# Retention then bilinear FFN: the query and key transposes of chunks 9 to 35 move from SP's DMA queue to the TensorE

## The chip, the core and the metric

One core of one Trainium2 chip. The metric is device microseconds of one execution, the median of several runs: 366.49 us for the kernel before (three runs, 366.24 to 366.78). Engines are named as the profile names them: PE is the TensorE (matmuls), PEld its weight loads, DVE the VectorE, ACT the ScalarE, POOL the GpSimd, SP the SyncE, whose queue only issues DMAs here.

## What is computed

A retention layer without softmax, then a bilinear feed-forward layer (FFN):

```python
# q, k, v: [8 batches, 8 heads, 576 positions, 64], float32
scores = 1/8 * q @ k^T                       # per batch and head
Dmat[h, i, j] = gamma_h ** (i - j) if i >= j else 0,  gamma_h = 1 - 2 ** (-5 - h)
x = ((scores * Dmat) @ v)  -> [4608 tokens, 512]      # heads side by side
out = ((x @ w_a) * (x @ w_b)) @ w_out        # 512 -> 1536 -> 512, float32
```

## The kernel before

The 4608 tokens are 36 chunks of 128. Two batches of 576 positions make nine chunks, so every fifth chunk is shared by two batches. The decay is split into a factor for the query (`qs`) and one for the key position (`vs`), so that a chunk needs only a causal mask and a running state `kv` of keys times values.

A chunk goes through these steps. `load` (L97) fetches q, k and v by SP DMAs. `cast` (L182) makes bf16 copies: q and k into the halves of one tile `qkb`, and v times `vs` into `vb` (L193). From chunk 4 on `cast` is called from `ahead`; for chunks 0 to 8 q and k are cast on ACT and DVE (L188, L189), for chunks 9 to 35 on POOL (L191, L192). The scores need q and k with the head dimension on the partitions, `qkT`. For chunks 0 to 8 `transposes` (L208) makes it on PE: eight 128x128 transposes into a PSUM tile `tp` (L213), whose halves ACT and DVE copy out (L217, L218). For chunks 9 to 35 `turn` (L200) makes it with one DMA transpose on SP's queue (L203). `state` (L225) adds keys times values to `kv` on PE (L236), and ACT copies the two diagonal blocks out (L241, L242). `scores` (L244) makes two PSUM tiles on PE (L253); the mask multiplication into `sT` on DVE (L259) is not issued at once but put in the list `later`. `outputs` (L267) multiplies `sT` and the state with `vb` and `qkT` on PE (L276, L285); the multiplication with `qs` into `xT` on DVE (L291) is put in `later` as well.

The FFN (`ffn_block`, L299) works on blocks of 512, 256, 384, 384 and then six times 512 tokens. For each of 12 column groups F it makes `pa` (L309, 4 matmuls, copied out by ACT as `ha`, L315) and `pb` (L322, 4 matmuls, multiplied by `ha` on DVE into `hT`, L327); then for each chunk of the block `po` (L335, 12 matmuls of 512 columns), copied out by ACT or DVE as `osb` (L344, L346) and stored by SP (L347). `pa`, `pb` and `po` share three PSUM buffers; `tp`, the scores and `o` share four.

The order of all instructions is written out by hand. `ffn_block` is a generator that yields after each matmul with a cost in units of one 512-column matmul; after each `pb` and at three places of each `po` it allows other work. After each `pb` and twice in each `po` it also calls `pop`, which issues one entry of `later`. A list `todo` of steps with due times in the same unit is worked off at these places. For chunks 9 to 35, taken in pairs, the due times are placed back from the block that needs the result (`starts`): `third` is at least 16 units ahead of it and 60 ahead of the next pair's. In the kernel before, `ahead` is due 104 units ahead of `third` (not before 176) and issues the casts of the pair, the loads of two chunks four further on, and the two DMA transposes; `first_stage` (`state` of the first chunk) 16 ahead of `second`; `second_stage` (`state` of the other and `scores` of both) 36 ahead of `third`, or 26 for chunks 9 and 10. Chunks 4 to 8 have their own times. At the end of each FFN block `flush` issues all that is left in `later`.

Of the kernel before, what the change touches and what calls it, by code (L numbers as in the profile page):

```python
# [11 lines left out]
BF16 = mybir.dt.bfloat16  # L12
# [6 lines left out]
def kernel(  # L19
# [19 lines left out]
    nc = tc.nc  # L39

    B, H, S, D = q.shape
    DM = H * D
# [4 lines left out]
    HP = H // 2  # L47
# [9 lines left out]
    def rows_of(i):  # L57

        b, m = 2 * (i // PER), i % PER
        if m < MID:  # L60
            return [(0, 128, b, 128 * m)]
        if m == MID:
            return [(0, 64, b, 128 * m), (64, 64, b + 1, 0)]
        return [(0, 128, b + 1, 64 + 128 * (m - MID - 1))]

    def pool(name, bufs, space=None):
        kw = {} if space is None else {"space": space}
        return ctx.enter_context(tc.tile_pool(name=name, bufs=bufs, **kw))
# [2 lines left out]
    big = pool("big", 1)  # L71
    stage = pool("stage", 5)
    nat = pool("nat", 5)
    qkt_pool = pool("qkt", 6)
    st_pool = pool("st", 4)
    h_pool = pool("hT", 2)
    ha_pool = pool("ha", 6)
# [19 lines left out]
    def load(i):  # L97
        if i >= NCH:
            return
        tiles = []  # L100
        for name, src in (("qf", q), ("kf", k), ("vf", v)):
            t = stage.tile([128, DM], FP32, tag=name, name=name)
            for r0, n, b, s0 in rows_of(i):
                nc.sync.dma_start(
                    t[r0:r0 + n, :].rearrange("p (h d) -> p h d", h=H),
                    src[b, :, s0:s0 + n, :].rearrange("h s d -> s h d"))
            tiles.append(t)
        staged[i] = tiles
# [62 lines left out]
    natural, transposed, kv_of, state_of, scored = {}, {}, {}, {}, {}  # L171
# [9 lines left out]

    def cast(i, early=False):  # L182
        qf, kf, vf = staged.pop(i)
        qkb = nat.tile([128, 2, DM], BF16, tag="qkb", name="qkb")
        vb = nat.tile([128, DM], BF16, tag="vb", name="vb")
        qb, kb = qkb[:, 0], qkb[:, 1]
        if early:
            nc.scalar.copy(qb, qf)  # L188
            nc.vector.tensor_copy(kb, kf)  # L189
        else:  # L190
            nc.gpsimd.tensor_copy(qb, qf)  # L191
            nc.gpsimd.tensor_copy(kb, kf)  # L192
        nc.gpsimd.tensor_tensor(  # L193
            vb.rearrange("p (h d) -> p h d", h=H),
            vf.rearrange("p (h d) -> p h d", h=H),
            vs[:, i % PER, :].unsqueeze(2).to_broadcast([128, H, D]),
            op=ALU.mult)
        natural[i] = (qkb, qb, kb, vb)

    def turn(i):  # L200

        qkT = qkt_pool.tile([128, 2, HP, 128], BF16, tag="qkT", name="qkT")
        nc.sync.dma_start_transpose(  # L203
            qkT.rearrange("p w c s -> p (w c) s"),
            natural[i][0].rearrange("p w d -> p (w d)"))
        transposed[i] = qkT

    def transposes(i, how):  # L208
        qkb, qb, kb, vb = natural[i]
        tp = ps_att.tile([128, 2, HP, 128], BF16, tag="att", name="tp")  # L210
        for w, src in ((0, qb), (1, kb)):
            for p in range(HP):
                nc.tensor.transpose(tp[:, w, p, :],  # L213
                                    src[:, p * 128:(p + 1) * 128], identity)
        qkT = qkt_pool.tile([128, 2, HP, 128], BF16, tag="qkT", name="qkT")
        if how == "both":
            nc.scalar.copy(qkT[:, 0], tp[:, 0])  # L217
            nc.vector.tensor_copy(qkT[:, 1], tp[:, 1])  # L218
        elif how == "act":
            nc.scalar.copy(qkT, tp)  # L220
        else:
            nc.vector.tensor_copy(qkT, tp)
        transposed[i] = qkT

    def state(i):  # L225
        m = i % PER
        if m == PER - 1:
            return
        qkb, qb, kb, vb = natural[i]
        r = slice(64, 128) if m == MID else slice(0, 128)  # L230
        if m == 0 or m == MID:
            kv_of[0] = ps_kv.tile([128, HP, 128], FP32, tag="kv", name="kv")
        kv = kv_of[0]
        for p in range(HP):
            sl = slice(p * 128, (p + 1) * 128)
            nc.tensor.matmul(kv[:, p, :], kb[r, sl], vb[r, sl],  # L236
                             start=(m in (0, MID) and p == 0), stop=True,
                             skip_group_check=True)
        st = states[i % len(states)]
        state_of[i + 1] = st  # L240
        nc.scalar.copy(st[0:64, :, 0:64], kv[0:64, :, 0:64])  # L241
        nc.scalar.copy(st[64:128, :, 64:128], kv[64:128, :, 64:128])  # L242
# [23 lines left out]

    def outputs(i):  # L267
        m = i % PER
        qkb, qb, kb, vb = natural.pop(i)
        qkT = transposed.pop(i)  # L270
        sT = scored.pop(i)
        o = ps_att.tile([128, HP, 128], FP32, tag="att", name="o")
        for p in range(HP):
            for hi in (0, 1):
                e0 = p * 128 + 64 * hi
                nc.tensor.matmul(o[64 * hi:64 * hi + 64, p, :],  # L276
                                 vb[:, e0:e0 + 64], sT[:, hi, p, :],
                                 start=(p == 0), stop=(m == 0),
                                 skip_group_check=True)
        if m > 0:  # L280
            st = state_of.pop(i)
            n = 64 if m == MID else 128
            for p in range(HP):
                for hi in (0, 1):
                    nc.tensor.matmul(o[64 * hi:64 * hi + 64, p, 0:n],  # L285
                                     st[:, p, 64 * hi:64 * hi + 64],
                                     qkT[:, 0, p, 0:n],
                                     start=False, stop=True,
                                     skip_group_check=True)
        s0 = rows_of(i)[0][3]  # L290
        later.append(lambda: nc.vector.tensor_tensor(  # L291
            xT[:, :, i * 128:(i + 1) * 128], o, qs[:, :, s0:s0 + 128],
            op=ALU.mult))
# [60 lines left out]
    make_qs(0)  # L354
    make_qs(1)
    cast(0, early=True)
    make_qs(2)
    for i in range(4):
        transposes(i, "both")
        if i == 0:  # L360
            make_qs(3)
        scores(i)
        state(i)
        flush()
        if i < 3:
            if i == 2:
                load_w(0, 128 * WCOLS[0])
            cast(i + 1, early=True)
        outputs(i)
        flush()  # L370
# [19 lines left out]
        at += total(n)  # L390

    counts = {"cast": 4, "load": 8}
    FIRST_TURNED = 9

    def ahead(upto, early=False):
        while counts["cast"] <= min(upto, NCH - 1):
            i = counts["cast"]
            cast(i, early)
            counts["cast"] += 1
            if counts["load"] < NCH:  # L400
                load(counts["load"])
                counts["load"] += 1
            if i >= FIRST_TURNED:
                turn(i)

    def first_stage(g):
        state(g[0])

    def second_stage(g):
        for i in g[1:]:  # L410
            state(i)
        for i in g:
            scores(i)

    def third_stage(g):
        flush()
        for i in g:
            outputs(i)

    def one_by_one(what, i):  # L420
        if what == "T":
            ahead(i, early=True)
            transposes(i, "both")
        elif what == "S":
            scores(i)
            state(i)
        else:
            flush()
            outputs(i)

    todo = []
    limit = 1e9
    for i in range(NCH - 1, 8, -2):
        g = (i, i + 1) if i + 1 < NCH else (i,)
        third = min(starts[i] - 16, limit - 60)
        limit = third
        second = third - (26 if i == 9 else 36)
        todo += [(max(176, third - 104), ahead, (g[-1],)),
                 (second - 16, first_stage, (g,)),
                 (second, second_stage, (g,)),  # L440
                 (third, third_stage, (g,))]
    for i, first, second, third in (
            (4, 117, 122, 129), (5, 134, 138, 143), (6, 147, 151, 158),
# [46 lines left out]
```

## Time and profile before

| | before |
|---|---|
| median of three runs | 366.49 us |
| the profiled execution's own time | 366.24 us |
| its span, first to last instruction | 364.5 us |
| PE busy | 335.3 us, 92% of the span |
| DVE, ACT, POOL busy | 164.0, 115.1, 77.5 us |
| mean granted PE clock | 0.99 |
| DMA transposes on SP's queue | 27, issued from 83.6 to 296.5 us |

A row of the profile's groups names line, engine, operation and tiles, then the busy time, the mean duration of one in ns, and after a bar the time that the engine sat idle before them with what ended that. Durations of matmuls overlap, since they are pipelined: what one costs in a stream is the distance from its start to the next one's, not its duration. In a timeline a row is the start, the time until the last of its instructions ends, and the instructions.

The profile divides at some 97 us. Ahead of that loads, casts and the first chunks wait for each other (PE is busy for 74 of 97 us, by its pipelined count). After that PE runs the FFN with the steps of the other chunks between its matmuls, up to 361 us, when the last copy and store follow.

### The profile page before, as it was taken

What the parts mean: (1) busy time and instruction counts of PE and PEld (TensorE: products, weight loads), DVE (VectorE), ACT (ScalarE), POOL (GpSimd) and SP (SyncE); (2) the same over time, 40 slices, a digit from 0 to 9 for tenths busy, and PEclk for the clock granted to TensorE, in tenths of its full rate; (3) what the DMA queues carried; (4) which work ended last, traced back from release to release, by engine and by line L of the source; (5) the groups of instructions that cost most, each with busy time, mean ns of one, the idle gap of its engine ahead of it and who ended that gap; (6) DMA issues with size and microseconds to landing.
All of it is one profiled execution on the core that took longest, in us unless ns stands there. A gap on an engine that the chain in (4) does not pass through costs nothing.

```text
span 364.5 us, 6162 instructions
## 1 busy us (share of the span) xinstructions
PE 335.3 (92%) x2390; PEld 174.8 (48%) x2424; DVE 164.0 (45%) x279; ACT 115.1 (32%) x234; POOL 77.5 (21%) x113
## 2 busy tenths in 40 slices
PE   2669998686999999999999999999999999999995
PEld 1444444464555566444444544454444544444442
DVE  4542343455266345436534643455345435523421
ACT  7323314242333234143314321332243133212320
POOL 3550022452240413402231313140403000000000
PEclk9999999699999999999999999999999999999999
DMA  9999899999996299595099419943980430011002
GB/s 173 182 203 208 162 194 252 219 184 186 227 216 110 82 199 221 107 215 47 18 228 267 67 40 239 237 64 76 259 159 0 92 112 2 0 59 58 0 31 86
DMA packets 151021, 49.95 MB, mean 137 GB/s; under 512 B 141776, under 2 KB 146384, under 8 KB 150992
## 3 DMA queue, kind: packets, MB, share of 16 engines
q1 hardware_dynamic: 146240, 44.84, 62.8%
q0 software_dynamic: 4752, 4.72, 8.2%
q8 instruction: 19, 0.31, 0.4%
q14 instruction: 10, 0.08, 0.1%
HBM read 37.75 MB, written 9.44 MB: 129 GB/s over the span
## 4 chain that ended last, share of the span: by engine, by line
PE 88%; DVE 7%; ACT 3%; issue 2%; DVEq 0%
PE pa L309 25%; PE po L335 25%; PE pb L322 24%; PE o L276 3%; DVE sT L259 3%; PE o L285 2%; PE kv L236 2%; PE tp L213 2%; ACT qkT L217 1%; DVE hT L327 1%; DVE qkT L218 1%; DVE osb L346 1%; DVE xT L291 1%; ACT qs L154 0%; DVE qkb L189 0%
## 5 line engine op out<-in xcount | busy, mean ns | idle before, releaser
L327 DVE TENSOR_TENSOR hT<-ha,pb 128x512 bf16<-128x512 bf16 (+2 forms) x120 | 76.0, 634 | 110.7 <-PE pb L322 100.7
L309 PE MATMUL pa<-xT,wa_sb 128*128 128x512 bf16 (+2 forms) x472 | 113.3, 364 | 2.4 <-DVE xT L291 1.6
L322 PE MATMUL pb<-xT,wb_sb 128*128 128x512 bf16 (+2 forms) x471 | 111.6, 360 | 0.7 <-DVE hT L327 0.3
L315 ACT CAST ha<-pa 128x512 bf16<-128x512 f32 (+2 forms) x120 | 65.1, 542 | 131.9 <-PE pa L309 119.4
L335 PE MATMUL po<-wo_sb,hT 128*128 128x512 bf16 x415 | 95.6, 379 | 1.4 <-issue 0.8
L193 POOL TENSOR_TENSOR vb<-vf,vs 128x512 bf16<-128x512 f32 x36 | 37.5, 1042 | 178.4 <-issue 83.0
L322 PEld LDWEIGHTS <-wb_sb 128*128 128x128 bf16 x480 | 47.4, 99 | 47.4 <-issue 0.5
L309 PEld LDWEIGHTS <-wa_sb 128*128 128x128 bf16 x480 | 45.7, 100 | 46.3 <-issue 3.9
L335 PEld LDWEIGHTS <-hT 128*128 128x128 bf16 x432 | 40.7, 98 | 47.2
L346 DVE COPY osb<-po 128x512 f32<-128x512 f32 x17 | 11.8, 691 | 57.6 <-PE po L335 57.6
L344 ACT COPY osb<-po 128x512 f32<-128x512 f32 x19 | 11.1, 585 | 70.1 <-PE po L335 69.0
L291 DVE TENSOR_TENSOR xT<-o,qs 128x512 bf16<-128x512 f32 x36 | 24.2, 685 | 9.6 <-PE o L285 8.4
L276 PE MATMUL o<-sT,vb 128*64 128x128 bf16 x288 | 16.7, 231 | 7.4 <-DVE sT L259 7.3
L191 POOL CAST qkb<-qf 128x512 bf16<-128x512 f32 x27 | 16.5, 610 | 21.2 <-PE kv L236 16.3
L276 PEld LDWEIGHTS <-vb 128*64 128x64 bf16 x288 | 11.0, 114 | 16.3 <-issue 13.1
L192 POOL CAST qkb<-kf 128x512 bf16<-128x512 f32 x27 | 16.6, 614 | 2.0 <-DMA kf<-in_k_dram 2.0
L213 PE MATMUL tp<-identity,qkb 128*128 128x128 bf16 x72 | 8.2, 270 | 8.1 <-ACT qkb L188 5.8
L253 PEld LDWEIGHTS <-qkT 64*128 64x128 bf16 x288 | 8.9, 99 | 10.6 <-DVE qkT L218 8.2
L236 PE MATMUL kv<-vb,qkb 128*128 128x128 bf16 (+1 forms) x128 | 13.5, 233 | 0.1
L236 PEld LDWEIGHTS <-qkb 128*128 128x128 bf16 (+1 forms) x128 | 9.6, 103 | 7.0 <-issue 1.4
L213 PEld LDWEIGHTS <-qkb 128*128 128x128 bf16 x72 | 5.6, 119 | 10.7 <-ACT qkb L188 7.2
L217 ACT COPY qkT<-tp 128x512 bf16<-128x512 bf16 x9 | 5.3, 585 | 13.4 <-PE tp L213 13.4
(193 smaller groups left out, 158.3 us busy)
## 6 DMA issues: line engine op xcount, KB each, us to landing
out_dram<-osb SPq DMA_DIRECT2D x36, 256.0 KB, 2.3
qf<-in_q_dram SPq DMA_DIRECT2D x32, 256.0 KB, 4.0
kf<-in_k_dram SPq DMA_DIRECT2D x32, 256.0 KB, 4.7
vf<-in_v_dram SPq DMA_DIRECT2D x32, 256.0 KB, 4.9
wo_sb<-in_moe_w_out_dram POOLq DMA_DIRECT2D x3, 512.0 KB, 17.8
qf<-in_q_dram SPq DMA_DIRECT2D x8, 128.0 KB, 3.7
kf<-in_k_dram SPq DMA_DIRECT2D x8, 128.0 KB, 4.2
vf<-in_v_dram SPq DMA_DIRECT2D x8, 128.0 KB, 4.6
```

Of the source, the lines that this page charges most:

```text
L191: nc.gpsimd.tensor_copy(qb, qf)
L192: nc.gpsimd.tensor_copy(kb, kf)
L193: nc.gpsimd.tensor_tensor(vb.rearrange("p (h d) -> p h d", h=H), vf.rearrange("p (h d) -> p h d", h=H), vs[:, i % PER, :].unsqueeze(2).to_ ...
L213: nc.tensor.transpose(tp[:, w, p, :], src[:, p * 128:(p + 1) * 128], identity)
L236: nc.tensor.matmul(kv[:, p, :], kb[r, sl], vb[r, sl], start=(m in (0, MID) and p == 0), stop=True, skip_group_check=True)
L276: nc.tensor.matmul(o[64 * hi:64 * hi + 64, p, :], vb[:, e0:e0 + 64], sT[:, hi, p, :], start=(p == 0), stop=(m == 0), skip_group_check=True)
L291: later.append(lambda: nc.vector.tensor_tensor(xT[:, :, i * 128:(i + 1) * 128], o, qs[:, :, s0:s0 + 128], op=ALU.mult))
L309: nc.tensor.matmul(pa[:, 0:n], wa_sb[:, c, fs], xT[:, c, tok0:tok0 + n], start=(c == 0), stop=(c == NC - 1))
L315: nc.scalar.copy(ha[:, 0:n], pa[:, 0:n])
L322: nc.tensor.matmul(pb[:, 0:n], wb_sb[:, c, fs], xT[:, c, tok0:tok0 + n], start=(c == 0), stop=(c == NC - 1))
L327: nc.vector.tensor_tensor(hT[:, F, 0:n], has[F][:, 0:n], pb[:, 0:n], op=ALU.mult)
L335: nc.tensor.matmul(po, hT[:, F, u * 128:(u + 1) * 128], wo_sb[:, F, :], start=(F == 0), stop=(F == NF - 1))
```

## The change

Chunks 9 to 35 take the way of the earlier ones: `turn` is gone, and `first_stage` calls `transposes` for both chunks of the pair, with "act" for the first and "dve" for the second, so that one engine copies a whole `tp` tile of 128x1024 (before, with "both", ACT and DVE took a 128x512 half each). `first_stage` also calls `ahead`, which now reaches two chunks further, to the end of the next pair. Its own due time stays 52 units ahead of `third` (36 for chunks 9 and 10, whose second stage moves from 26 to 20 units ahead). q and k get tiles of their own in place of `qkb`, and the `qkt` pool has four buffers in place of six.

```diff
-    qkt_pool = pool("qkt", 6)
+    qkt_pool = pool("qkt", 4)
...
     def cast(i, early=False):
         qf, kf, vf = staged.pop(i)
-        qkb = nat.tile([128, 2, DM], BF16, tag="qkb", name="qkb")
-        vb = nat.tile([128, DM], BF16, tag="vb", name="vb")
-        qb, kb = qkb[:, 0], qkb[:, 1]
+        qb, kb, vb = (nat.tile([128, DM], BF16, tag=t, name=t)
+                      for t in ("qb", "kb", "vb"))
...
-    def turn(i):
-
-        qkT = qkt_pool.tile([128, 2, HP, 128], BF16, tag="qkT", name="qkT")
-        nc.sync.dma_start_transpose(
-            qkT.rearrange("p w c s -> p (w c) s"),
-            natural[i][0].rearrange("p w d -> p (w d)"))
-        transposed[i] = qkT
...
-    FIRST_TURNED = 9

     def ahead(upto, early=False):
         while counts["cast"] <= min(upto, NCH - 1):
-            i = counts["cast"]
-            cast(i, early)
+            cast(counts["cast"], early)
             counts["cast"] += 1
             if counts["load"] < NCH:
                 load(counts["load"])
                 counts["load"] += 1
-            if i >= FIRST_TURNED:
-                turn(i)

     def first_stage(g):
+        ahead(g[-1] + 2)
+        for i, how in zip(g, ("act", "dve")):
+            transposes(i, how)
         state(g[0])
...
-        second = third - (26 if i == 9 else 36)
-        todo += [(max(176, third - 104), ahead, (g[-1],)),
-                 (second - 16, first_stage, (g,)),
-                 (second, second_stage, (g,)),
+        first = third - 36 if i == 9 else third - 52
+        todo += [(first, first_stage, (g,)),
+                 (third - (20 if i == 9 else 36), second_stage, (g,)),
                  (third, third_stage, (g,))]
```

## The prediction

> **What bounds the kernel now.** I read the page first: PE's share, then the chain that ended last.
>
> ```profile
> PE 335.3 (92%) x2390; PEld 174.8 (48%) x2424; DVE 164.0 (45%) x279; ACT 115.1 (32%) x234; POOL 77.5 (21%) x113
> PE 88%; DVE 7%; ACT 3%; issue 2%; DVEq 0%
> ```
>
> The chain is PE's own work for 88%. An average says nothing about a stage, so next the busy time by windows (us, PE busy, PEld, DVE, ACT, POOL, clock, DMA share, GB/s) and PE's waits in the same stretch.
>
> ```profile
> 97.00:361.00 264.00, 261.27 (x1821) 131.94 (x1848) 121.62 (x192) 79.80 (x158) 46.09 (x64) 1.00 0.58 115
> ...
> PE po L335 <- issue: 0.8, 5, 0.2
> PE pa L309 <- issue: 0.3, 2, 0.2
> PE pb L322 <- DVE hT L327: 0.3, 1, 0.3
> ```
>
> From 97 to 361 us PE is busy for 261.3 of 264.0 us at full clock, and no wait names a DMA: the transposes on SP's queue, though all 27 are used here, never hold PE. So in this stretch the kernel is PE's instruction stream, and whatever is put into it moves the end one for one. The price of what is put in is read where the kernel already does it, in chunks 4 to 8 (start, time until the last ends, instructions):
>
> ```profile
> 60.41 0.61 PE L213 MATMUL tp<-identity,qkb 128*128 128x128 bf16 x8
> 60.86 1.03 PE L335 MATMUL po<-wo_sb,hT 128*128 128x512 bf16 x4
> ...
> 77.43 0.62 PE L213 MATMUL tp<-identity,qkb 128*128 128x128 bf16 x8
> 77.89 0.60 PE L309 MATMUL pa<-xT,wa_sb 128*128 128x256 bf16 x4
> ```
>
> From the first transpose to the next matmul's start is 0.45 and 0.46 us for eight: 0.455 us a chunk, 57 ns each. The 0.61 is pipelined duration and not the cost.
>
> **What the Trainium skill says.** "TensorE: Matmul & The Clock Gate", section "Wait — 56ns, not 53.3ns?", gives 55.6 ns between warm 128-column matmuls and 215.7 ns for 512 columns. The trace agrees: 57 ns here, and 0.865 us for four 512-column matmuls. The same page, "Part 4: PE-mode transpose", says that the result lands in PSUM and needs a copy, and gives about 275 ns for a transpose in one kernel's context. The trace has 219 to 314 ns as duration, but 57 ns as distance; the measured distance decides. "VectorE: DVE Perf Modes", "Why PSUM operands drop a tier": a bf16 copy from PSUM can run at twice the plain rate. Agrees: 425 ns (L218) against 691 ns for a float32 copy of the same 512 columns (L346). The first page again, "Part 1: The HAM clock gate": an idle window of some 3.4 us halves PE's clock. The trace has one such stretch, granted 0.50 from 67.26 to 74.09 us, after PE stood mostly idle from 63.6 to 67.1.
>
> **Part by part.** I compared both kernels' instruction orders engine by engine. PE's differ in two things only: 27 blocks of eight transposes, placed in front of the `state` of each pair, and a move for chunks 9 and 10.
>
> *Added on PE.* 27 x 8 = 216 transposes. For chunks 11 to 35, 25 x 0.455 = 11.4 us, all on the path. Bounds: 0.44 us a chunk (twice the 0.22 to 0.23 of four `kv` matmuls of the same shape) and 0.46, so 11.0 to 11.5. No gap of switching is added: such gaps, 0.09 us, stand in front of the score and output matmuls with 64-wide tiles, and none in front of 128x128 `kv` or `tp`.
>
> *Chunks 9 and 10.* Here DVE sets the end of a short stretch:
>
> ```profile
> 98.96 0.81 PE L309 MATMUL pa<-xT,wa_sb 128*128 128x384 bf16 x4
> 99.16 0.69 DVE L346 COPY osb<-po 128x512 f32<-128x512 f32 x1 [5.20 <-PE po L335]
> ...
> 101.57 0.68 DVE L259 TENSOR_TENSOR sT<-sc_1201,mask 128x512 bf16<-128x512 f32 x1
> 102.16 1.01 DVE L327 TENSOR_TENSOR hT<-ha,pb 128x384 bf16<-128x384 bf16 x2
> 102.76 0.81 PE L322 MATMUL pb<-xT,wb_sb 128*128 128x384 bf16 x4 [0.31 <-DVE hT L327]
> ```
>
> `osb`, four masks at 0.60 and `hT` run in a row, and PE waits until 102.76; by its own work (five groups of 0.65 from 98.96) it would be there at 102.2, 0.55 earlier. In the changed order the scores (0.87 us of PE from 97.22 to 98.09) come behind the last four `po` matmuls, not ahead of them. So `po` ends 0.91 - 0.87 = 0.04 later in spite of the 16 transposes, DVE's row starts 0.04 later, and `hT` frees the buffer at 102.8. PE's own work, two pairs of `pa` and `pb` and a third `pa`, then reaches the same `pb` at 102.2 + 0.91 = 103.1. That is +0.36, since the 0.55 of waiting is used up. I take 0.36; the bounds are 0.0 (DVE's row ends it still) and 0.91.
>
> *Added on ACT and DVE.* 14 copies of 128x1024 on ACT, 13 on DVE. ACT's row is not in the trace; its `ha` copies take 373, 478 and 585 ns for 256, 384 and 512 columns, 0.83 ns a column, so 1.01 us (estimate; upper bound 2 x 585 = 1.17). DVE: 425 + 512 x 0.52 = 0.69 (the difference of 425 and 691 is what 512 columns cost at the double rate; upper bound 0.85). Queued behind ACT's copy are the two state copies (365 ns each) and the next `ha`. Counting from the end of `pb`: `tp` is done at 0.455, ACT sees it 0.2 later, copies until 1.67, the states until 2.40, `ha` until 2.99 (512 columns) or 2.88 (384). The `pb` that needs its buffer starts at 1.14 + 3 x 0.865 = 3.73 or 1.14 + 3 x 0.65 = 3.09. Slack is 0.7 and 0.2 us: nothing on the path. With the upper bound the 384 blocks, two pairs, just touch. DVE has only the copy between an `hT` and the next, 1.73 us apart and now 1.14 more. I take 0; range 0 to 0.5 us in all. PSUM: `tp` takes two of four buffers whose last readers were the previous pair's masks, issued ahead of its outputs, so nothing waits.
>
> *The new wait on POOL's casts.* In front of the transposes PE waits for the pair's q and k, and all the FFN is queued behind. POOL's instruction order is unchanged, and POOL runs ahead: chunk 10's last cast starts at 72.75 us, and PE comes to it at about 93.8; chunk 12's at 81.25 against some 107. Later the casts hang on buffers freed three pairs earlier. Cost 0; if the cover were gone, 2.3 us of POOL a chunk (610 + 614 + 1042 ns) would show.
>
> *Removed from SP.* 27 issues and their transfers:
>
> ```profile
> L203 SPq DMA_TRANSPOSE qkT<-qkb  x27: 1247/2225/4124, 83.6 to 296.5; - x27
> DMA to landing us min/median/max: 3.0/4.5/6.6
> ```
>
> Some 27 x 2.2 = 60 us of a queue that PE doesn't wait for. `ahead` moves later for chunks 9 and 10 and takes four chunks' casts and loads at once; the loads stay in order, their buffers are freed by casts long done, and the stores between them have four `osb` buffers. Nothing on the path before, so nothing gained. Nothing up to 83.6 us changes in any queue, so the opening with its slow-clock stretch stays.
>
> *Sum.* 11.4 + 0.36 = 11.7 us. On the profiled execution: span 364.5 + 11.7 = 376.2, own time 366.24 + 11.7 = 377.9. The median stands 0.25 above that execution: 366.49 + 11.7 = 378.2.
>
> **Rivals.**
>
> (1) The copies become a bound. For: ACT has 1.7 us of copies at one edge. Against: the slack above. If each of 13 pairs lost 0.5 us beyond the slack: 378.2 + 6.5 = 384.7.
>
> (2) A second slow-clock stretch, if PE must wait at a first stage for casts. The known one is 6.83 us at half clock, so it costs some 3.4: 381.6. Against: the lead of 20 us.
>
> (3) The slow-clock stretch of the opening goes away by a small shift: 378.2 - 3.4 = 374.8. Against: that stretch lies ahead of the first changed instruction.
>
> (4) Faster than before: the DMA transposes slow PE's matmuls by their traffic, and without them the stream runs quicker. It decides if the slowing is over 11.7 / 264 = 4.4% of PE's stretch. If it were 5.5%, 14.5 us come back: 363.7. Against: four matmuls take 0.86 us at 198 to 204 us, among DMA transposes, and 0.86 at 340 to 350, long after the last one.
>
> That the change does not do what it says is excluded by the instruction order.
>
> **Numbers.** Forecast 0.80, rivals (1) 0.05, (2) 0.06, (3) 0.05, (4) 0.02; the rest, 0.02, is small change around zero and a little below. Two parts in a thousand, 0.7 us, are about what measurements of this kernel can tell from no change. The forecast's own span: 11.0 + 0.0 to 11.5 + 0.9 + 0.5, that is 377.5 to 379.4, and 0.5 on both sides for the runs: 377.0 to 379.9. To hold 8 in 10 I reach up to rival (2) and a little down: 376.5 to 381.9. Slower 0.97, same 0.01, faster 0.02.
>
> **What would show it.** PE's count rises by 216 matmuls, and each pair's 16 transposes take 0.91 us from first start to the next `kv`. PE's waits after 97 us stay below 1 us a kind, none of them on ACT's or DVE's `qkT`. The `pb` at 102.76 starts near 103.1. ACT's new rows show 1.0 us, DVE's 0.7. I would be wrong if transposes in this stream lie further apart than 57 ns, if `pa` and `pb` show waits on `ha` or `hT` after each first stage, or if the pace of `pa` and `pb` differs from 0.865.

## Result, and the profile after

The changed kernel takes 376.87 us (median of four runs, 376.60 to 378.66), beside 366.63 us for the kernel before (four runs, 366.24 to 367.12): a ratio of 1.0289, 95% interval 1.0254 to 1.0324. It is slower, by about what was forecast: the median lies 1.3 us below the 378.2 us of the forecast, and 0.1 us below the forecast's own span of 377.0 to 379.9, but inside the stated range of 376.5 to 381.9. The profiled execution took 377.08 us, its span is 375.4 us.

First the same two lines of the page as before, PE's share and the chain that ended last.

```profile
PE 345.6 (92%) x2604; PEld 186.4 (50%) x2640; DVE 172.5 (46%) x292; ACT 127.9 (34%) x248; POOL 77.8 (21%) x113
PE 78%; DMA 7%; SPq 6%; DVE 3%; issue 2%; POOL 1%; ACT 1%; DVEq 0%
```

PE has 2604 recorded instructions in place of 2390, 214 more, where 216 were added (some records can be missing). The 7% DMA and 6% SPq in the chain are no new bound. They lie ahead of 60 us: in this execution the chain runs through the loading of q, k, v and `wo_sb` there. Another execution of the same kernel (e8 below) has 86% PE and 1% each of DMA and SPq, with the same span within 0.2 us. Then the stretch in which PE had been the bound, by windows (us, PE busy, PEld, DVE, ACT, POOL, clock, DMA share, GB/s), here up to 372 us:

```profile
97.00:372.00 275.00, 271.40 (x2019) 143.25 (x2048) 129.78 (x204) 91.72 (x171) 46.25 (x64) 1.00 0.40 88
```

And PE's waits from 99 to 372 us:

```profile
PE po L326 <- issue: 1.6, 10, 0.2
PE pa L300 <- issue: 0.6, 4, 0.2
```

PE is still busy for 271.4 of 275.0 us at full clock. No wait names a copy, a cast or a DMA, and the wait of the `pb` on `hT` has gone from the list. The 1.6 us at `po` are above the 1 us a kind that the prediction allowed. They are ten pieces of at most 0.2 us for which the profile shows no cause, and they cannot add much: 200 transposes at 55.6 ns (below) are 11.12 us of the 11.17 that this stretch grows by. The DMA share fell from 0.58 to 0.40. Here is what PE does at the place that the prediction worked out, and at the first pair of transposes after it (start, time until the last ends, instructions):

```profile
101.62 0.81 PE L300 MATMUL pa<-xT,wa_sb 128*128 128x384 bf16 x4
102.26 0.81 PE L313 MATMUL pb<-xT,wb_sb 128*128 128x384 bf16 x4
...
106.41 0.39 PE L204 MATMUL tp<-identity,qb 128*128 128x128 bf16 x4
106.63 0.39 PE L204 MATMUL tp<-identity,kb 128*128 128x128 bf16 x4
106.86 0.39 PE L204 MATMUL tp<-identity,qb 128*128 128x128 bf16 x4
107.08 0.39 PE L204 MATMUL tp<-identity,kb 128*128 128x128 bf16 x4
107.30 0.39 PE L227 MATMUL kv<-vb,kb 128*128 128x128 bf16 x4
107.53 0.81 PE L300 MATMUL pa<-xT,wa_sb 128*128 128x384 bf16 x4
```

From the first transpose to `kv` is 0.89 us for 16, that is 55.6 ns each. The two copies that ACT and DVE got (busy us and mean ns, then idle time):

```profile
L211 ACT COPY qkT<-tp 128x1024 bf16<-128x1024 bf16 x14 | 14.2, 1012 | 11.4 <-PE tp L204 11.4
L213 DVE COPY qkT<-tp 128x1024 bf16<-128x1024 bf16 x13 | 8.9, 686 | 4.7 <-PE tp L204 4.0
```

To say where the time went, I cut both executions at the same instructions: the last 256-wide `pb` of the third FFN block (A), the third 384-wide `pb` of the next block (B, the one that had waited), the start of the last `osb` copy (C), and the end of the span.

| us | before | after | difference |
|---|---|---|---|
| start to A | 92.24 | 91.32 | -0.92 |
| A to B | 10.52 | 10.94 | +0.42 |
| B to C | 258.13 | 269.30 | +11.17 |
| C to the end | 3.65 | 3.82 | +0.17 |
| span | 364.54 | 375.38 | +10.84 |

So the two parts that the change touches make 11.59 us of the difference. Up to A PE's instructions are the same in both kernels, and yet this part differs by 0.92 the other way. Experiment e7 takes up the reason.

The kernel before has runs from 364.69 to 367.94 us (68 of them beside the experiments, median 365.38; the median of the four in the first comparison lay 1.2 us above that), so comparisons with few runs sit up to a microsecond apart, and I read the small experiments from these cuts.

### The profile page after: what moved, and what is told of

Same layout as the page of the kernel before. It is cut to its first block, busy times and chain, and to the rows that moved or that the text cites. A ratio compares the mean times of both kernels' runs of the same rounds, so it can differ in the third digit from the quotient of the medians.

```text
span 375.4 us, 6629 instructions
## 1 busy us (share of the span) xinstructions
PE 345.6 (92%) x2604; PEld 186.4 (50%) x2640; DVE 172.5 (46%) x292; ACT 127.9 (34%) x248; POOL 77.8 (21%) x113
## 4 chain that ended last, share of the span: by engine, by line
PE 78%; DMA 7%; SPq 6%; DVE 3%; issue 2%; POOL 1%; ACT 1%; DVEq 0%
PE po L326 23%; PE pa L300 22%; PE pb L313 21%; SPq L104 6%; DMA wo_sb<-in_moe_w_out_dram 5%; PE tp L204 4%; PE o L267 3%; DMA vf<-in_v_dram 3%; PE kv L227 2%; PE o L276 2%; DVE sT L250 1%; DVE hT L318 1%; ACT qkT L208 1%; DVE qkT L209 0%; POOL wa_sb L163 0%
## 5 line engine op out<-in xcount | busy, mean ns | idle before, releaser
L326 PE MATMUL po<-wo_sb,hT 128*128 128x512 bf16 x414 | 94.5, 379 | 2.0 <-issue 1.6
L267 PE MATMUL o<-sT,vb 128*64 128x128 bf16 x288 | 16.7, 231 | 7.6 <-DVE sT L250 7.4
L190 POOL CAST qb<-qf 128x512 bf16<-128x512 f32 x27 | 16.7, 618 | 23.1 <-issue 18.4
L204 PE MATMUL tp<-identity,qb 128*128 128x128 bf16 x144 | 15.0, 231 | 6.2 <-ACT qb L187 6.2
L191 POOL CAST kb<-kf 128x512 bf16<-128x512 f32 x27 | 16.6, 613 | 8.7 <-DVE hT L318 4.0
L211 ACT COPY qkT<-tp 128x1024 bf16<-128x1024 bf16 x14 | 14.2, 1012 | 11.4 <-PE tp L204 11.4
L204 PE MATMUL tp<-identity,kb 128*128 128x128 bf16 x144 | 15.1, 232 | 1.5 <-DVE kb L188 1.5
L204 PEld LDWEIGHTS <-qb 128*128 128x128 bf16 x144 | 10.5, 102 | 11.1 <-ACT qb L187 7.4
L227 PE MATMUL kv<-vb,kb 128*128 128x128 bf16 (+1 forms) x128 | 13.3, 230 | 0.0
```

What stands on the lines that cost most here:

```text
L204: nc.tensor.transpose(tp[:, w, p, :], src[:, p * 128:(p + 1) * 128], identity)
L227: nc.tensor.matmul(kv[:, p, :], kb[r, sl], vb[r, sl], start=(m in (0, MID) and p == 0), stop=True, skip_group_check=True)
L267: nc.tensor.matmul(o[64 * hi:64 * hi + 64, p, :], vb[:, e0:e0 + 64], sT[:, hi, p, :], start=(p == 0), stop=(m == 0), skip_group_check=True)
L326: nc.tensor.matmul(po, hT[:, F, u * 128:(u + 1) * 128], wo_sb[:, F, :], start=(F == 0), stop=(F == NF - 1))
```

## Experiments

My theory was the forecast's: PE's stream pays for each transpose, and nothing else pays or gains. The rivals were that the copies pay a part, that taking the DMA transposes away gives a part back, that the opening moves, and that the move of the second stage of chunks 9 and 10 matters. The cuts A, B and C are those of the table.

**e1: no transposes at all.** Chunks 9 to 35 use one constant tile as `qkT`. It leaves out these transposes and copies, by DMA as well as by PE, and so that part of the computation.

```diff
+    still = const.tile([128, 2, HP, 128], BF16, name="still")
...
-        for i, how in zip(g, ("act", "dve")):
-            transposes(i, how)
+        for i in g:
+            transposed[i] = still
```

> The changed kernel without any transposes for chunks 9 to 35: their scores and state products read one constant tile in place of qkT, so this part is not computed. Theory (the added time is PE's 216 transposes, and the DMA transposes had cost nothing): the kernel before less at most 0.6 us of the wait at chunks 9 and 10, some 366.1 us, and in the profile the same pace behind 97 us as before. Rival A (DMA transposes had slowed the kernel, so taking them away gave some 1.5 us back and the PE transposes cost more than 11.7): 364.5 to 365.

Measured: 364.9 us (20 runs), ratio 0.9983 (0.9969 to 0.9997). As a time this falls into what I had given to rival A, 364.5 to 365, since I had counted from 366.5 us; the kernel before took 365.4 beside it, and the difference is the 0.5 us of the theory. The pace decides. The windows from B to C, first of the kernel before, then of the changed one, then of e1:

```profile
102.76:360.89 258.13, 255.82 (x1775) 128.83 (x1803) 117.91 (x186) 77.84 (x154) 46.09 (x64) 1.00 0.56 114
```

```profile
102.26:371.56 269.30, 266.14 (x1975) 140.16 (x2003) 125.35 (x198) 90.03 (x167) 46.25 (x64) 1.00 0.38 85
```

```profile
101.01:359.13 258.12, 255.82 (x1776) 128.97 (x1803) 117.56 (x185) 78.29 (x154) 45.99 (x64) 1.00 0.39 90
```

The kernel before, with its DMA transposes (DMA share 0.56), and e1, without any (0.39), need the same 258.1 us. The DMA transposes cost PE nothing, and so rival (4) has nothing to give back. Nor does the rest of the change, which e1 keeps (separate tiles for q and k, the smaller `qkt` pool, the later casts and loads), cost anything behind B. The changed kernel has 200 more matmuls (1975 against 1775) and 11.17 us more: 55.8 ns each. e1's half microsecond against the kernel before lies from A to B (10.05 against 10.52 us), where it has the later second stage without the transposes.

**e2: both ways at once.** The kernel before, DMA transposes kept, with 16 transposes on PE ahead of each pair's `state`, which nobody reads and nobody copies out.

```diff
     def first_stage(g):
+        for i in g:
+            unread(i)
         state(g[0])
```

> The kernel before with all its DMA transposes, plus 16 PE transposes ahead of each pair's state into a PSUM tile that nobody reads and nobody copies. Theory: 25 x 0.4536 + 0.91 for chunks 9 and 10, whose stages stay where they were, so 12.2 us over the kernel before, 378.8. Rival A: DMA transposes cost 1.5 us beside it, which stays in: 378.8 too, but then the run without any transposes is 1.5 below. Rival B (the copies out of PSUM carry part of the cost): 3 us or more below 378.8.

Measured: 378.76 us, ratio 1.0348 (1.0311 to 1.0386), the time expected, but 13.4 us above the 365.4 of the kernel before beside it, where 12.2 had been expected. By the cuts A to C it is 12.3 us more than before. B to C:

```profile
104.09:373.38 269.29, 266.14 (x1973) 140.15 (x2003) 117.56 (x186) 77.63 (x153) 46.33 (x64) 1.00 0.55 108
```

269.29 us with neither ACT's nor DVE's copies (ACT busy for 77.6 us, not 90.0) and with the DMA traffic, 269.30 in the changed kernel with the copies and without the traffic. Together with e1, which showed the traffic to be free, this puts both side terms at zero to 0.01 us, and the whole price is PE's. e2 is 1.6 us slower than the changed kernel in span: 1.10 from start to A, in which the two openings differ, and 0.73 from A to B (11.67 against 10.94), which e5 explains, less 0.2 in the tail.

**e3: PE's transposes twice.**

```diff
-        for w, src in ((0, qb), (1, kb)):
+        for w, src in ((0, qb), (1, kb)) * (2 if i > 8 else 1):
```

> The changed kernel with each PE transpose of chunks 9 to 35 made twice into the same tile, the copies once. Theory: 216 more at 56 ns, 12.1 us over the changed kernel, 389.0. Rival B (copies): 3 us or more below that.

Measured: 389.26 us, ratio 1.0651 (1.0617 to 1.0684). B to C:

```profile
103.73:384.19 280.46, 277.89 (x2169) 151.27 (x2203) 125.80 (x198) 91.17 (x167) 46.66 (x64) 1.00 0.36 81
```

The second set costs 280.46 - 269.30 = 11.16 us, the first cost 11.17. The price is linear; there is no slack that the first set used up.

**e4: the copies twice.**

```diff
             nc.scalar.copy(qkT, tp)
+            nc.scalar.copy(qkT, tp)
         else:
             nc.vector.tensor_copy(qkT, tp)
+            nc.vector.tensor_copy(qkT, tp)
```

> The changed kernel with the copy of each qkT of chunks 9 to 35 made twice in a row, 1.01 us more on ACT or 0.7 us more on DVE, 27 times. Theory: the first copy costs nothing; the second uses up the slack that was worked out, 0.7 us with 512 columns and 0.2 with 384, so up to 0.3 us a pair, in all 0 to 4 us over the changed kernel and the waits to be seen at pa and pb. Rival B (the copies already cost something): some 13 us more, one copy's length a pair.

Measured: 381.72 us, ratio 1.0442 (1.0406 to 1.0477); B to C 273.29 us, 3.99 more than the changed kernel, 0.3 us a pair, the upper end of what was expected. The timeline of e4 at the first pair after B:

```profile
107.36 1.01 ACT L211 COPY qkT<-tp 128x1024 bf16<-128x1024 bf16 x1 [0.62 <-PE tp L204]
...
108.41 1.01 ACT L212 COPY qkT<-tp 128x1024 bf16<-128x1024 bf16 x1
...
109.31 0.36 ACT L234 CAST state<-kv 64x256 bf16<-64x256 f32 x1
...
109.69 0.37 ACT L235 CAST state<-kv 64x256 bf16<-64x256 f32 x1
110.08 0.86 ACT L308 CAST ha<-pa 128x384 bf16<-128x384 f32 x2
...
110.61 0.81 PE L315 MATMUL pb<-xT,wb_sb 128*128 128x384 bf16 x4 [0.67 <-ACT ha L308]
```

This is the queue that the prediction laid out: behind the copies stand two state copies and `ha`, and `pb` stands behind `ha`. With one copy, slack covers it (e2). With a second 1.01 us, PE waits 0.67 here. So rival (1) names a real limit, less than one more copy away, and the changed kernel stays inside it. The loss a pair is smaller with 512-wide blocks; in the pair near 202 us `pb` comes 0.3 us late.

**e5: the move of chunks 9 and 10 undone.**

```diff
-                 (third - (20 if i == 9 else 36), second_stage, (g,)),
+                 (third - (26 if i == 9 else 36), second_stage, (g,)),
```

> The changed kernel with the second stage of chunks 9 and 10 back at 26 units ahead of the third, so that their scores come ahead of the last four po matmuls again. Theory: the DVE row that frees the FFN buffer starts 0.87 us later, PE waits there again, and from the last po matmuls' start the pb in question comes 0.45 us later than in the changed kernel; within the scatter in the time. Rival: no change at that place.

Measured: 378.11 us, ratio 1.0352 (1.0325 to 1.0379). B to C is unchanged at 269.29 us; A to B is 11.67 us, 0.73 more, where 0.45 had been expected. DVE's row does come later by what was expected (the first `hT` 10.81 us after A, 9.93 in the changed kernel), but it is not what holds `pb`. The timeline of e5:

```profile
101.19 0.81 PE L300 MATMUL pa<-xT,wa_sb 128*128 128x384 bf16 x4
101.70 1.01 DVE L318 TENSOR_TENSOR hT<-ha,pb 128x384 bf16<-128x384 bf16 x2
102.03 0.48 ACT L306 CAST ha<-pa 128x384 bf16<-128x384 f32 x1 [0.90 <-PE pa L300]
102.56 0.81 PE L313 MATMUL pb<-xT,wb_sb 128*128 128x384 bf16 x4 [0.57 <-ACT ha L306]
```

Here `pb` starts 0.05 us after the end of the `ha` copy (102.03 + 0.48 = 102.51) of the `pa` directly ahead of it, and PE stands still meanwhile. In the kernel before it starts 0.05 after the first `hT` (102.16 + 0.55 = 102.71). So the same `pb` waits for another reader, as if it had been given another of the three PSUM buffers. That is read from start times alone and not shown. e2, which keeps the 26 too, shows the same 11.67 and the same wait on `ha`. The move thus avoids 0.73 us of waiting, without which the change would cost that much more.

**e6: the move alone, in the kernel before.**

```diff
-        second = third - (26 if i == 9 else 36)
+        second = third - (20 if i == 9 else 36)
...
-                 (second - 16, first_stage, (g,)),
+                 (third - (42 if i == 9 else 52), first_stage, (g,)),
```

> The kernel before with only this part of the change: second stage of chunks 9 and 10 at 20 units ahead. Theory: PE's wait of 0.31 us at pb is gone, and from 92.2 us on the kernel is 0.5 us ahead; 366.1 us if the opening's half-clock stretch is of the same length. Rival: the wait only moves, 366.6.

Measured: 365.1 us (20 runs), ratio 1.0 (0.9987 to 1.0014). A to B is 10.28 us, 0.24 less than before, half of what I expected. The DVE row did come early, but in this version the third `pa` starts at 101.73, 0.96 us after the `pb` ahead of it and so 0.31 late, and 0.04 after the end of the first `hT`: part of the wait moved one group of matmuls ahead and did not go.

**e7: the opening's slow-clock stretch filled.** The kernel before, with unread matmuls around the outputs of chunk 5, where PE had stood mostly idle.

```diff
             flush()
+            if i == 5:
+                idle_work(6)
             outputs(i)
+            if i == 5:
+                idle_work(3)
```

`idle_work` makes that many 512-column matmuls of `wa_sb` and `xT` into a PSUM tile `pw` that nobody reads.

> The kernel before with nine matmuls of 512 columns put into PE's idle time at the end of the first FFN block (six ahead of chunk 5's outputs, three behind), whose result nobody reads. Theory (the half-clock stretch near 67 to 74 us comes from PE's idle time just ahead of it, and its length, 0, 3.4 or 6.8 us, makes the scatter between runs): the stretch is gone, the granted clock is 1.00 in every run, and the time is up to 3 us below the kernel before, 363.5 to 365.5. Rival (the stretch comes from elsewhere): 366.5 to 368, with the nine matmuls partly on the path.

The reason for it: the windows show one half-clock stretch in the opening of each execution, but not of one length. Before, then after:

```profile
67.26:74.09 6.83, 6.10 (x40) 3.89 (x39) 2.02 (x4) 2.28 (x6) 3.03 (x5) 0.50 0.98 217
```

```profile
68.46:71.88 3.42, 3.10 (x19) 1.86 (x17) 1.18 (x3) 1.76 (x4) 1.48 (x2) 0.51 1.16 224
```

Among the profiled executions without a filler the stretch is 6.83 us in five (before, e2, e3, e4, e6) and 3.41 in four (after, e1, e5, e8), that is one or two steps of 3.41. The mean clocks of the runs without a profile say the same: 3.41 us at half clock in some 365 take 0.005 off the mean, 6.83 take 0.009, and of the kernel before's 68 runs 18 have 0.990 or 0.991, 35 have 0.995 and 11 have 0.999 or 1.000, while of the changed kernel's ten three have 0.989 or 0.990, five 0.995 and two 0.998 or 1.000. By this reading both lengths, and none at all, occur in both kernels. With the filler it is gone from the opening of e7:

```profile
64.52 1.46 PE L423 MATMUL pw<-xT,wa_sb 128*128 128x512 bf16 x5
...
67.20 0.82 PE L423 MATMUL pw<-xT,wa_sb 128*128 128x512 bf16 x3
68.05 0.60 PE L309 MATMUL pa<-xT,wa_sb 128*128 128x256 bf16 x4
```

The `pa` matmuls behind it take 0.60 us, at full clock, against 0.91 in the kernel before at 67.11. Measured: 364.37 us (12 runs), ratio 0.997 (0.9953 to 0.9988), and 1.06 us less from start to A. That is not yet the price of the stretch, for the two openings differ ahead of it as well. From chunk 5's transposes to chunk 7's, with the stretch between them, is 15.03 us in e7, against 17.02 before (60.41 and 77.43, shown in the prediction):

```profile
61.34 0.61 PE L213 MATMUL tp<-identity,qkb 128*128 128x128 bf16 x8
...
76.37 0.62 PE L213 MATMUL tp<-identity,qkb 128*128 128x128 bf16 x8
```

All five executions with 6.83 us of half clock take 16.7 to 17.0 us here, the four with 3.41 take 15.5 to 15.7, and e7 and e9 with none 15.0 and 14.7. So the long stretch costs about 2 us and the short one about 0.7, not the 3.4 that I had priced for rival (3): at full clock PE is busy for only 6.7 of 9 us at this place (67 to 76 us in e7), so part of what half speed takes would have been waiting. The medians differ by only 1.0 us, as they would if the runs of the kernel before are a mix with the long stretch, the short one and none.

The other difference lies ahead. The trace's clock records begin with the change to full clock, at 29.7 us before and at 31.5 in e7, and between 29.1 and 31.5 in all executions but e10's. In each of these the half-clock stretch, where there is one, starts 37.55 us later. Chunk 5's transposes start at 60.1 to 61.3 us, half a microsecond later for each microsecond by which the full clock comes later. The changed kernel's profile has both: full clock 1.15 us later (30.86), which puts chunk 5 back by 0.63, and the short stretch, which saves 1.55. Together that is the -0.92 of the table.

**e8: the changed kernel again**, without an edit, beside more runs of the kernel before.

> The changed kernel once more, beside many runs of the kernel before on the same chip. Theory (PE's added time is 11.2 us behind the stage of chunks 9 and 10, plus 0.4 there, and the rest of any difference is the length of the half-clock stretch in the opening, which both kernels draw at random): the medians differ by 11.3 to 11.8 us, more than the 10.2 of the first comparison. Rival (the changed kernel really opens 1 us faster): 10.2 again.

Measured: 378.05 us (six runs, 376.79 to 379.80) beside 365.46 us (14 runs of the kernel before), ratio 1.0353 (1.0327 to 1.0379). The first comparison gave +10.2 us, this one +12.6, above what I expected; the two intervals do not touch. The cuts are the same in both executions: 10.94 and 269.29 us here, 10.94 and 269.30 first. The rival, that the changed kernel really opens a microsecond faster, would have given 10.2 again; these runs do not support it. All ten runs of the changed kernel have a median of 377.5, 12.1 above the 365.4 of the kernel before.

**e9: e6 and e7 together.**

The edit is the two of e6 and e7.

> The kernel before with both small gains: second stage of chunks 9 and 10 at 20 units ahead, and the nine filling matmuls at the end of the first block. Theory: 0.24 us below the run with the filling matmuls alone, 364.1, no half-clock stretch, and some 1.2 us below the kernel before.

Measured: 364.01 us (nine runs), ratio 0.9955 (0.9937 to 0.9974). A to B 10.29, B to C 258.13 us; the gain is e7's and the 0.24 of e6.

**e10: e9 with a warm start.** In chunks 0 to 3 PE waits for ACT and DVE between short bursts. Unread 128-column matmuls on the identity fill these gaps: 28 ahead of the first transposes, 12 behind each chunk's transposes and 4 ahead of its outputs.

```diff
+    early_work(28)
     for i in range(4):
         transposes(i, "both")
+        early_work(12)
...
+        early_work(4)
         outputs(i)
```

> As the one with both gains, plus filling 128x128 matmuls on the identity in the first 26 us: 28 ahead of the first transposes, 12 behind each of the first four chunks' transposes, four ahead of their outputs. Theory: if PE's idle time keeps the clock at half in the opening, the first transposes take 0.45 us in place of 1.0 and each of the four chunks is some 0.7 us quicker, 361 to 362.5. Rival: the share of work in a chunk is still too small to raise the clock, or the fill is in the way, 364 to 366.

Measured: 360.42 us (five runs, 358.73 to 360.81), ratio 0.985 (0.9827 to 0.9873), more gain than expected, and the fastest kernel here. The profiled execution is the fastest of the five. The transposes of chunk 1 in e9, then in e10:

```profile
10.18 1.03 PE L213 MATMUL tp<-identity,qkb 128*128 128x128 bf16 x8
11.26 0.59 ACT L217 COPY qkT<-tp 128x512 bf16<-128x512 bf16 x1 [1.13 <-PE tp L213]
...
12.36 0.61 PE L253 MATMUL sc<-qkT 64*128 64x128 bf16 x8 [1.14 <-DVE qkT L218]
```

```profile
9.74 0.62 PE L213 MATMUL tp<-identity,qkb 128*128 128x128 bf16 x8
10.20 0.83 PE L361 MATMUL pw<-identity 128*128 128x128 bf16 x12
10.40 0.58 ACT L217 COPY qkT<-tp 128x512 bf16<-128x512 bf16 x1 [0.71 <-PE tp L213]
...
11.50 0.40 PE L253 MATMUL sc<-qkT 64*128 64x128 bf16 x8 [0.47 <-DVE qkT L218]
```

From the start of the transposes to ACT's copy is 1.08 us in e9 and 0.66 in e10. Chunks 1 and 2 start their transposes 5.1 us apart in e9 (10.18, 15.29) and 4.07 in e10 (9.74, 13.81), and A is reached at 84.98 us, against 90.72. The windows show a clock of 1.00 in both from 9 to 20 us, but this column says nothing there: it takes time without a record for full clock, and the first clock record begins at 31.36 us in e9's trace and at 7.06 in e10's. The matmuls agree with the records. In e9, the first `pa` matmuls of 512 columns in the FFN lie 425 ns apart up to 31.39 us (ten in 4.25 us), the `pb` behind them 216:

```profile
27.14 4.41 PE L309 MATMUL pa<-xT,wa_sb 128*128 128x512 bf16 x10 [0.22 <-issue]
31.39 2.75 PE L322 MATMUL pb<-xT,wb_sb 128*128 128x512 bf16 x12
```

So without the filler PE ran at half pace for the first 31 us, the start of the FFN included, and with it for the first 7.

## Why the prediction was right, and where its terms were off

The mechanism was right: PE's own stream, priced by the distance between starts, is what the change costs.

*Chunks 11 to 35.* Forecast 11.4 us, measured 11.17. The 0.455 us for eight came from chunks 4 to 8, where each end is read to 0.01 us over eight instructions only; over 200 it is 0.447, 55.8 ns each. e1, e2 and e3 show that this is the whole of it. The Trainium skill's page "TensorE: Matmul & The Clock Gate", section "Wait — 56ns, not 53.3ns?", has 55.6 ns for a warm 128-column matmul; the transposes in this stream keep that distance, while each one's duration is 219 ns.

*Chunks 9 and 10.* Forecast +0.36, measured +0.42. The prediction said that DVE's row would start 0.04 later and PE would arrive behind it. Counted from A, `osb` starts at 6.92 us before and 6.93 after, and the first `hT` at 9.92 and 9.93; the `pb` no longer waits for it. The transposes took 0.88 from A to the first 384-wide `pa` (7.60 against 6.72 us), not 0.91. The term that was mis-sized is the 0.55 of waiting that was to be used up: it was 0.46 (3.34 us from that `pa` to B, against 3.80). "Five groups of 0.65" is 3.25; the third `pa` is held 0.08 more. Both before and after it starts 0.05 us after the second `ha` ends (101.11 + 0.48 = 101.59, start 101.64; 101.09 + 0.48 = 101.57, start 101.62), so PE has this wait in both kernels.

*Copies, casts and SP.* All were put at 0, and all are 0: the copies by e2, the removed DMA transposes by e1 and e2, POOL's casts by the list of waits after 99 us. The copies' durations, 1012 and 686 ns, match the estimates of 1.01 and 0.69 us. The slack that the prediction worked out for ACT holds: the first copy is free, the second in e4 is not.

*The opening.* "Nothing up to 83.6 us changes" holds for PE's instructions, yet the prediction's "so the opening with its slow-clock stretch stays" was too strong. This execution has the stretch at half its length and reaches A 0.92 us sooner. By the mean clocks of the runs both lengths occur in both kernels, so this is put down to the spread of executions and not to the change; among the profiled ones the kernel before's opening had only the long stretch. Nor was this stretch PE's only slow time, as the prediction had it: e9 and e10 show half pace for about the first 30 us too, which both kernels share. The later full clock and the shorter stretch (e7) are also why the measured difference of these two profiled executions is 10.84 and not 11.59.

*The sum.* 11.17 + 0.42 = 11.59 us, against 11.7 forecast. On the median of the runs shown, 366.49, it gives 378.1; the four runs came to 376.87, and the six of e8 to 378.05. That the absolute time of e8 fits so well is in part luck: the 366.49 that it starts from lies 1.1 us above the median of the later 68 runs. The difference is the surer test, and over all runs it is 12.1 us against 11.7.

*Rivals.* (1) did not happen, and e4 shows its threshold. (2) did not happen: the clock from 97 us on is 1.00. (3) happened by half in the profiled execution, and its price was mis-sized: I took half speed over 6.83 us as 3.4 us lost, and e7 and e9 show about 2 for all of it. (4) fell with e1: 258.12 against 258.13 us.

*What stays open.* The difference was 10.2 us in the first comparison and 12.6 in the second. I attribute that to the openings, which differ from execution to execution. But the length of the slow stretch does not sort the runs fully: runs of the kernel before with the same mean clock of 0.995 lie both near 365 and near 367 us. The moment at which the full clock comes differs too, by up to 2.4 us in the profiled executions, and does not enter the mean clock; whether it explains these runs is not settled, since for runs without a profile only the mean clock is on record. And the sharing of PSUM buffers behind e5 and e6 is argued from start times, not shown.

## What to carry to other kernels

Where one engine is busy for 99% of a long stretch, price what is put into its queue by the distance between starts, times the count. Then ask only whether the other engines' queues still meet their slack; here a DMA that nobody waited for gave nothing back when it was removed. Look for gains where that engine is not full: the same 365 us held some 5 us in the opening, which filler matmuls brought out, and none in the stretch that the change touched.

## What the runs showed of the hardware

- 27 DMA transposes or none, 0.56 or 0.39 of DMA share: PE's stream takes 258.13 and 258.12 us. Nothing of that traffic reaches the matmuls.
- Half-clock stretches came in lengths of 3.41 and 6.83 us, after PE had been mostly idle for 3.5 us (busy for 1.0 us from 63.6 to 67.1 us in the kernel before). They cost about 0.7 and 2 us. The Trainium skill's page "TensorE: Matmul & The Clock Gate", "Part 1: The HAM clock gate", speaks of a window of some 3.4 us, and the lengths fit it. Nine extra matmuls in the gap removed the stretch.
- At the start PE ran at half pace: ten 512-column matmuls took 4.25 us up to 31.39 us in e9, where the first clock record begins at 31.36. Unread matmuls that kept PE busy from 2.4 us on brought full pace at 7.06 us (eight transposes then took 0.62 us and not 1.03), and with the gains of e9 the kernel was 1.5% faster than before.
